# Sliding-window attention with a SwiGLU block: V loads of the opening issued behind a mask matmul, two V copies moved to VectorE

## The chip, the cores and the metric

The kernel runs on one core of a Trainium2 chip. The metric is the device time of one execution in microseconds (us). The core has TensorE (PE, matrix products), VectorE (DVE), ScalarE (ACT), GpSimd (POOL) and SyncE (SP), and 16 DMA engines that all queues share.

## The reference

```python
# q, k, v: [8, 8, 576, 64] float32 (batch, head, position, head dim)
scores = (1/8) * q @ k^T
mask   = (rel >= 0) & (rel < 64)          # rel = query position - key position
attn   = softmax(where(mask, scores, -1e9))
x      = (attn @ v) -> [4608 tokens, 512]  # tokens = batch * position, heads side by side
g      = x @ w_gate                        # [512, 1536]
out    = (g * sigmoid(g) * (x @ w_val)) @ w_out   # [1536, 512], float32
```

Each query sees its own and the 63 positions before it.

## The kernel before

The 4608 tokens are 36 chunks of 128. For each chunk n the kernel forms scores (S), takes the exponential (ACT, tile `pt`), masks, multiplies with V (AV, tile `va`), normalises (DVE, tiles `rc` and `xb`) and transposes the result into `xT` (X). Four chunks make one FFN chunk of 512 tokens: F c.f computes one 128-column group of the gate and value products with `Wg` and `Wv` (L788), tanh on ACT (`sig`, L794), and two DVE operations (`uu` L796, `hT` L798); O multiplies with `Wo` (L819).

The program is recorded as a list of operations (`_Graph.op`), each put on an engine in the order of the Python calls. `emit` then gives every engine its list and adds a semaphore wait wherever an operation reads or overwrites what another one made. So each engine runs strictly in the order of the calls. `after=` adds a wait on one more operation; `self.hold`, if set, is passed as `after` to the K, Q and V loads. Behind the opening, a written-out order (`EARLY`, `LOADS`, `SHIPS`) and a planner that picks PSUM banks take over.

All casting loads (float32 in DRAM, bf16 in SBUF) are issued from POOL: `load2` (K and Q of two chunks, L376), `load` (V, K or Q of one chunk, L367), `load_w` (two 128-column groups of a weight, L382). POOL also runs the masks' `affine_select` and some copies.

`shift(n, r, eng)` (L296 through `copy`) is the V copy of the change: the attention of chunk n needs the last 64 rows of V of the chunk before and the first 64 of its own in one tile, in the order of the scores' rows. `shift(n, r)` copies 64 rows of `va[n]` into tile `vs[n + r - 1]`: r=1 the later half for the next chunk, r=0 the first half for the chunk itself. AV of chunk 1 reads vs 0 (`shift(0,1)` and `shift(1,0)`), that of chunk 2 vs 1 (`shift(1,1)`, `shift(2,0)`), that of chunk 3 vs 2 (`shift(2,1)`, `shift(3,0)`).

`Sbias` (L449) is a pair of matmuls that puts a large negative number into the masked places of a chunk's scores, ahead of the score matmuls (`Sb`, L469 and L473). `warm` (L763) are matmuls on zeros. In the opening (`loads`, then `build` up to `self.main("F0.2-3b")`) the order is written out by hand: loads and masks, first transposes of K and Q, chunks 0 to 3 of the attention, and the first FFN groups in halves of 256 tokens.

Of the kernel before, what the change touches and what calls it, by code (L numbers as in the profile page):

```python
# [166 lines left out]
class _Kernel:  # L167
# [235 lines left out]
    def T2(self, st, x, engs):  # L403
        g = self.g
        src = (self.ks2 if x == "k" else self.qs2)[st % 2]
        dst = self.kT if x == "k" else self.qT
        z0 = (2 * st) % self.NZ
        for cc in range(2):
            bank, bk = self.bank("a")
            tb = bank[:, 0:256].bitcast(BF).rearrange("p (c j t) -> p c j t", c=2, j=2)  # L410

            def pe(e, cc=cc, tb=tb):
                for c in range(2):
                    for j in range(2):
                        for p in range(2):
                            r = e.transpose(tb[64 * p:64 * p + 64, c, j, :], src[:, 4 * cc + 2 * c + p, j, :], self.ident[:, :])  # L416
                return r

            g.op("pe", pe, reads=["ident", ("s2", x, st % 2, 0), ("s2", x, st % 2, 1)], writes=[bk])
            d = dst[:, 2 * cc:2 * cc + 2, 128 * z0:128 * z0 + 256].rearrange("p c (t j) -> p c t j", j=2)  # L420
            a = tb.rearrange("p c j t -> p c t j")
            self.copy(engs[cc], d, a, [bk], [(x + "T", z, cc) for z in (z0, z0 + 1)])
            self.drop([(bank, bk)])
# [282 lines left out]
    def X(self, n, eng="sp", kind="f", half=False):  # L706
        if n >= NCH:
            return
        g = self.g
        ix, it, u = n % 4, (n // 4) % self.NX, n % 4  # L710
        xb = self.xb[ix]
        xo = self.xT[it][:, :, 128 * u:128 * u + 128]
        xk = [("xb", ix, 0), ("xb", ix, 1)]
        if eng == "sp":
            g.op("sp", lambda e: e.dma_start_transpose(xo, xb[:, :]), reads=xk, writes=[("xT", it, u)], dma=True)
            return
        bank, bk = self.bank(kind)
        tb = bank[:, 0:256].bitcast(BF).rearrange("p (c t) -> p c t", c=4)

        def pe(e):  # L720
            for c in range(4):
                for p in range(2 if half else 1):
                    w = 64 if half else 128
                    r = e.transpose(tb[w * p:w * p + w, c, :], xb[:, 128 * c + w * p:128 * c + w * p + w], self.ident[:, :])  # L724
            return r

        g.op("pe", pe, reads=["ident"] + xk, writes=[bk])
        self.copy(eng, xo, tb, [bk], [("xT", it, u)])
        self.drop([(bank, bk)])
# [38 lines left out]
    def F(self, c, fs, lo=0, hi=512):  # L768
        g = self.g
        nf, n = len(fs), hi - lo  # L770
        w = nf * n
        xT = self.xT[c % self.NX]
        xk = [("xT", c % self.NX, u) for u in range(lo // 128, hi // 128)]
        ih = c % self.NH
        i = self.n_s % self.NS
        self.n_s += 1
        sig, uu = self.sig[i], self.uu[i]
        out = self.hT[ih][:, fs[0]:fs[0] + nf, lo:hi]
        v3 = lambda a: a[:, 0:w].rearrange("p (f t) -> p f t", f=nf)
        bs = []  # L780
        for W, wk in ((self.Wg, "Wg"), (self.Wv, "Wv")):
            bank, bk = self.bank("f")
            bs.append((bank, bk))

            def pe(e, W=W, bank=bank):
                for a, f in enumerate(fs):
                    for kk in range(NK):
                        r = e.matmul(bank[:, a * n:a * n + n], W[:, kk, f * 128:f * 128 + 128], xT[:, kk, lo:hi],  # L788
                                     start=(kk == 0), stop=(kk == NK - 1))
                return r  # L790

            g.op("pe", pe, reads=xk + [(wk, f) for f in fs], writes=[bk], cost=w * 0.0017)
            if wk == "Wg":
                g.op("act", lambda e, G=bank: e.activation(sig[:, 0:w], G[:, 0:w], ACTF.Tanh, scale=0.5), reads=[bk], writes=[("sig", i)])  # L794
        (G, gk), (V, vk) = bs
        g.op("dve", lambda e: e.scalar_tensor_tensor(uu[:, 0:w], sig[:, 0:w], 1.0, G[:, 0:w], ALU.add, ALU.mult),  # L796
             reads=[("sig", i), gk], writes=[("uu", i)])
        g.op("dve", lambda e: e.scalar_tensor_tensor(out, v3(uu), 0.5, v3(V), ALU.mult, ALU.mult),  # L798
             reads=[("uu", i), vk], writes=[("hT", ih, f) for f in fs])
        self.drop(bs)  # L800
# [61 lines left out]
    def loads(self):  # L862
        self.first_loads()
        self.load2(0, "q")
        self.load2(1, "k")
        self.load2(1, "q")
        self.init()
        self.init_ident()
        self.init_mask()
        self.init_nmask()  # L870
        for n in range(4):
            self.load(n, "v")
        self.W(0, 2)
        self.load_w("g", 2, 4)
        self.shift(0, 1, "pool")
        self.shift(1, 1, "pool")
        self.load_w("v", 2, 4)
        self.shift(2, 1, "pool")
        self.shift(3, 0, "pool")
        self.W(4, 6)  # L880
        self.W(6, 8)
# [179 lines left out]
    def build(self):  # L1061
        F, S, AV, X, T2, O = self.F, self.S, self.AV, self.X, self.T2, self.O
        self.loads()
        self.banks("a", [4, 5, 6, 7, 0, 1, 2, 3, 4, 5, 0, 1, 2, 3, 4, 5, 6, 7, 0, 1, 2, 3, 4, 5, 6, 7, 6, 7])
        self.warm(48, n=121)
        self.first_T(("dve", "act"))
        s0 = self.Sa(0)
        T2(0, "q", ("act", "dve"))
        self.Sbias(s0)
        self.warm(2)  # L1070
        self.Sb(s0)
        s1 = self.Sa(1, True)
        self.Sb(s1)
        T2(1, "k", ("dve", "act"))
        T2(1, "q", ("dve", "act"))
        self.start()
        s2, s3 = self.Sa(2), self.Sa(3)
        a0, a1, a2, a3 = self.AVa(0), self.AVa(1), self.AVa(2), self.AVa(3)
        self.AVs(a0)
        self.shift(1, 0, "dve")  # L1080
        self.AVn(a0)
        self.shift(2, 0, "dve")
        self.Sbias(s2)
        self.Sb(s2)
        self.AVs(a1)
        self.AVn(a1)
        self.Sbias(s3)
        self.Sb(s3)
        X(0, "dve", "a")
        X(1, "dve", "a")  # L1090
        self.warm(1, j=2)
        self.AVs(a2)
        self.AVn(a2)
        self.AVs(a3)
        self.AVn(a3)
        F(0, (0, 1), 0, 256)
        X(2, "act", "a")
        X(3, "act", "a")
        F(0, (2, 3), 0, 256)
        F(0, (0, 1), 256, 512)  # L1100
        for n in range(4):
            self.did |= {w % n for w in ("s%d", "a%d", "x%d", "Tk%d", "Tq%d")}
        self.main("F0.2-3b")
        self.free = set(range(8))
        self.g.now = dict.fromkeys(self.g.now, max(self.g.now.values()))
        for t in self.program():
            self.pump()
            first = len(self.g.ops)
            self.main(t)
            self.at[t] = next((o for o in self.g.ops[first:] if o.eng == "pe"), None)  # L1110
        self.pump()
        assert not any(self.queues)
        self.g.emit()
# [42 lines left out]
```

## Time and profile before

| what | value |
|---|---|
| median of three runs | 329.18 us (328.08 to 330.15) |
| the profiled execution | 327.34 us, span 325.6 us |
| PE busy | 316.7 us, 97% of the span |
| DVE, ACT, POOL busy | 62%, 42%, 33% |
| casting loads (software queue) | 18.62 MB written |
| HBM read, written | 37.75 MB, 9.44 MB |
| granted TensorE clock | 1.00 |

The span runs from the first to the last instruction of the profiled execution; the execution's time has 1.74 us around it. PE's busy share counts pipelined matmuls as busy, so 97% does not say that PE is at its peak, but that there is little time in which nothing runs on it. In the timeline a row gives start, duration, engine, line, operation, output and input; a bracket gives the idle time before it and what ended it. For a DMA issued by POOL the row is the time that POOL takes to issue it; the data land some microseconds later (the DMA view has this).

### The profile page before, as it was taken

How to read it: one execution, taken by the hardware profiler on the slowest of the kernel's cores; microseconds unless marked ns; L12 is line 12 of the kernel's file. 1: busy time of each engine (PE TensorE's matmuls, PEld its weight loads, DVE VectorE, ACT ScalarE, POOL GpSimd, SP SyncE). 2: the span in 40 equal slices, each digit the busy share in tenths (PEclk: the TensorE clock that was granted, in tenths of full speed). 3: DMA queues.
4: the chain of work that ended last, by engine and by line, in shares of the span. 5: the costliest groups of instructions: out<-in, count | busy, mean ns of one | idle time of the engine just before them, and what ended most of it. 6: DMA issues, size and time to landing. Idle time of an engine off the chain costs nothing.

```text
span 325.6 us, 8009 instructions
## 1 busy us (share of the span) xinstructions
PE 316.7 (97%) x3415; PEld 171.1 (53%) x3451; DVE 203.5 (62%) x351; ACT 135.8 (42%) x243; POOL 108.3 (33%) x138
## 2 busy tenths in 40 slices
PE   7999999999999999999999999999999999999996
PEld 7584578775455445545444454545454544444443
DVE  4777978745387819675757575666656566555520
ACT  2745864454454344342434252525252532322222
POOL 8999980007930502506060607060702000000000
PEclk9999999999999999999999999999999999999999
DMA  9999999999999993949697999999996202100012
GB/s 146 178 193 184 168 166 154 130 169 182 166 175 140 168 197 80 125 100 138 122 133 113 142 120 123 137 121 126 121 138 81 66 35 56 42 32 33 34 62 99
DMA packets 161571, 39.85 MB, mean 122 GB/s; under 512 B 148608, under 2 KB 157056, under 8 KB 161536
## 3 DMA queue, kind: packets, MB, share of 16 engines
q0 software_dynamic: 111056, 18.62, 78.6%
q1 hardware_dynamic: 45024, 11.22, 24.5%
q10 hardware_dynamic: 5456, 9.51, 8.7%
q8 instruction: 27, 0.44, 0.6%
q14 instruction: 8, 0.07, 0.1%
HBM read 37.75 MB, written 9.44 MB: 145 GB/s over the span
## 4 chain that ended last, share of the span: by engine, by line
PE 92%; ACT 3%; issue 2%; POOL 1%; DVE 1%; ACTq 0%; POOLq 0%
PE ps L788 56%; PE ps L819 28%; PE ps L642 3%; ACT pt L481 1%; PE ps L506 1%; PE ps L724 1%; PE ps L469 1%; PE ps L844 1%; PE ps L416 1%; POOL qs L376 1%; PE ps L473 1%; PE ps L593 1%; ACT kT L294 0%; ACT qT L294 0%; PE ps L510 0%
## 5 line engine op out<-in xcount | busy, mean ns | idle before, releaser
L796 DVE SCALAR_TENSOR_TENSOR uu<-sig,ps 128x512 bf16<-128x512 bf16 x108 | 73.9, 684 | 64.3 <-ACT sig L794 63.8
L788 PE MATMUL ps<-xT,Wv 128*128 128x512 bf16 (+1 forms) x486 | 110.5, 351 | 0.5
L788 PE MATMUL ps<-xT,Wg 128*128 128x512 bf16 (+1 forms) x479 | 107.8, 351 | 2.7 <-issue 1.9
L794 ACT ACTIVATE sig<-ps 128x512 bf16<-128x512 f32 x108 | 65.0, 602 | 76.2 <-PE ps L788 76.0
L819 PE MATMUL ps<-Wo,hT 128*128 128x512 bf16 x413 | 94.5, 379 | 0.5 <-issue 0.2
L798 DVE SCALAR_TENSOR_TENSOR hT<-uu,ps 128x512 bf16<-128x512 bf16 x108 | 74.2, 687 | 3.7
L788 PEld LDWEIGHTS ps<-xT,Wv 128*128 128x128 bf16 x496 | 48.5, 98 | 44.9
L367 POOL DMA_DIRECT2D kn<-in_k_dram x31 | 27.6, 894 | 127.4 <-PE ps L819 96.3
L788 PEld LDWEIGHTS ps<-xT,Wg 128*128 128x128 bf16 x496 | 46.6, 98 | 42.1 <-ACT pt L518 0.2
L819 PEld LDWEIGHTS ps<-Wo,hT 128*128 128x128 bf16 x420 | 41.0, 98 | 48.4
L826 ACT ACTIVATE ost<-ps 128x512 f32<-128x512 f32 x35 | 20.9, 597 | 88.6 <-PE ps L819 88.6
L367 POOL DMA_DIRECT2D va<-in_v_dram x40 | 35.5, 911 | 11.0 <-PE ps L819 10.9
L367 POOL DMA_DIRECT2D qn<-in_q_dram x31 | 27.9, 909 | 0.0
L669 DVE RECIPROCAL rp<-ps 128x14 f32<-128x14 f32 (+1 forms) x28 | 5.7, 203 | 31.6 <-PE ps L642 31.4
L481 ACT ACTIVATE pt<-ps 128x512 bf16<-128x512 f32 x36 | 18.9, 599 | 6.4 <-PE ps L473 6.0
L518 ACT ACTIVATE pt<-ps 128x512 bf16<-128x512 f32 x36 | 18.6, 603 | 4.3 <-PE ps L510 4.3
L671 DVE TENSOR_TENSOR xb<-ps,rp 128x896 bf16<-128x896 f32 (+1 forms) x28 | 19.4, 691 | 1.0
L642 PEld LDWEIGHTS ps<-va,pt 64*64 64x64 bf16 x888 | 10.8, 107 | 6.1 <-issue 5.5
L642 PE MATMUL ps<-va,pt 64*64 64x65 bf16 x888 | 13.4, 193 | 0.1
L527 DVE TENSOR_TENSOR pt<-pt,kmask 128x1024 bf16<-128x1024 bf16 x18 | 12.3, 684 | 0.0
L527 DVE TENSOR_TENSOR pt<-pt,mask 128x1024 bf16<-128x1024 bf16 x14 | 9.4, 686 | 0.9 <-ACT pt L481 0.9
L473 PE MATMUL ps<-qT,kT 64*64 64x64 bf16 x288 | 7.8, 195 | 0.0
(65 smaller groups left out, 139.4 us busy)
## 6 DMA issues: line engine op xcount, KB each, us to landing
out_dram<-ost ACTq DMA_DIRECT2D x35, 256.0 KB, 3.2
va<-in_v_dram POOLq DMA_DIRECT2D x32, 128.0 KB, 5.9
kn<-in_k_dram POOLq DMA_DIRECT2D x25, 128.0 KB, 5.3
qn<-in_q_dram POOLq DMA_DIRECT2D x25, 128.0 KB, 5.7
Wg<-in_moe_w_gate_dram POOLq DMA_DIRECT2D x6, 256.0 KB, 7.1
Wv<-in_moe_w_val_dram POOLq DMA_DIRECT2D x6, 256.0 KB, 7.1
Wo<-in_moe_w_out_dram POOLq DMA_DIRECT2D x2, 768.0 KB, 19.0
qs<-in_q_dram POOLq DMA_DIRECT2D x3, 256.0 KB, 6.2
```

What stands on the lines that cost most here:

```text
L367: self.g.op("pool", lambda e, d=d, a=a: e.dma_start(d, a), writes=ks, dma=True, after=self.hold)
L481: g.op("act", lambda e, po=po, p=p: e.activation(po, sv[p], ACTF.Exp, scale=SCALE), reads=[bx[p][1]], writes=[pk[p]])
L518: g.op("act", lambda e, po=po, p=p: e.activation(po, sv[p], ACTF.Exp, scale=SCALE), reads=[bx[p][1]], writes=[pk[p]])
L527: self.g.op("dve", lambda e: e.tensor_tensor(pt, pt, m, ALU.mult), reads=pk + [key], writes=pk)
L642: z = e.matmul(self.psa[64 * c:64 * c + 64, o:o + 65], pt[p][rows, h, 64 * a:64 * a + 64], va[m][rows, h, 0:65], start=first, stop=phase = ...
L671: g.op("dve", lambda e, d=d, num=num, rb=rb: e.tensor_tensor(d, num, rb, ALU.mult), reads=bk + [("rp", k)], writes=xk, cost=(1.0, 0.25)[k])
L788: r = e.matmul(bank[:, a * n:a * n + n], W[:, kk, f * 128:f * 128 + 128], xT[:, kk, lo:hi], start=(kk == 0), stop=(kk == NK - 1))
L794: g.op("act", lambda e, G=bank: e.activation(sig[:, 0:w], G[:, 0:w], ACTF.Tanh, scale=0.5), reads=[bk], writes=[("sig", i)])
L796: g.op("dve", lambda e: e.scalar_tensor_tensor(uu[:, 0:w], sig[:, 0:w], 1.0, G[:, 0:w], ALU.add, ALU.mult), reads=[("sig", i), gk], writes ...
L798: g.op("dve", lambda e: e.scalar_tensor_tensor(out, v3(uu), 0.5, v3(V), ALU.mult, ALU.mult), reads=[("uu", i), vk], writes=[("hT", ih, f) ...
L819: r = e.matmul(OB[:, :], hT[:, f, 128 * u:128 * u + 128], self.Wo[:, f, :], start=(f == 0), stop=(f == NF - 1), skip_group_check=mid is no ...
L826: g.op("act", lambda e: e.activation(ost[:, :], OB[:, :], ACTF.Copy), reads=[ok], writes=[("ost", io)])
```

## The change

V of chunks 2 and 3 and the weight loads are no longer issued with the other loads, but from a new function `next_loads`, which is called right behind `Sbias` of chunk 0. The load of V 2 gets this operation as `after`, so POOL waits there for the mask matmuls of chunk 0; what POOL issues behind it comes later in its list. `shift(0,1)` and `shift(2,1)` move from POOL to DVE, at two places in the hand-written order. The weights' order stays: columns 0-1, 2-3 and so on, gate ahead of value.

```diff
@@ loads
         self.init_nmask()
-        for n in range(4):
-            self.load(n, "v")
+        self.load(0, "v")
+        self.load(1, "v")
+
+    def next_loads(self, after):
+        self.hold = after
+        self.load(2, "v")
+        self.hold = None
+        self.load(3, "v")
         self.W(0, 2)
-        self.load_w("g", 2, 4)
-        self.shift(0, 1, "pool")
         self.shift(1, 1, "pool")
-        self.load_w("v", 2, 4)
-        self.shift(2, 1, "pool")
+        self.W(2, 4)
         self.shift(3, 0, "pool")
         self.W(4, 6)
         self.W(6, 8)
@@ build
         self.Sbias(s0)
+        self.next_loads(self.g.ops[-1])
         self.warm(2)
...
         self.AVs(a0)
+        self.shift(0, 1, "dve")
         self.shift(1, 0, "dve")
         self.AVn(a0)
...
         X(0, "dve", "a")
+        self.shift(2, 1, "dve")
         X(1, "dve", "a")
```

## The prediction

> **What bounds the kernel now.** I read the page first, then the chain of waits, then the timeline of the first 25 us, then the DMA view issue by issue.
>
> ```profile
> span 325.6 us, 8009 instructions
> ...
> PE   7999999999999999999999999999999999999996
> ...
> DMA  9999999999999993949697999999996202100012
> ...
> PE 92%; ACT 3%; issue 2%; POOL 1%; DVE 1%; ACTq 0%; POOLq 0%
> ```
>
> TensorE (PE) is on 92% of the chain that ended last, so a change counts only where PE has to start something later or may start it earlier. The DMA engines are at 9 in the first fifteen slices (about 120 us): early on there is a second queue that can become the bound. The edited code works before 25 us, so that is the stage to read. The chain there:
>
> ```profile
> 9.57 2.06 ACT pt L481 x4
> 11.64 0.49 ACT kT L294
> 12.13 0.50 ACT qT L294
> 12.67 0.22 PE ps L469
> ...
> 15.51 0.76 PE ps L593 x31
> 16.27 1.85 PE ps L788 x16
> 18.12 0.45 PE ps L724 x8
> 18.57 5.24 PE ps L788 x48
> ```
>
> ScalarE's exponentials and copies set the pace to 12.6 us; the attention of chunks 2 and 3 (L593) ends at 16.2; from there PE runs the first FFN groups (L788) without a gap. What GpSimd (POOL) does meanwhile:
>
> ```profile
> 5.38 3.79 POOL L367 DMA_DIRECT2D va<-in_v_dram  x4
> 9.14 0.78 POOL L382 DMA_DIRECT2D Wg<-in_moe_w_gate_dram  x1
> 9.88 0.78 POOL L382 DMA_DIRECT2D Wv<-in_moe_w_val_dram  x1
> 10.62 0.79 POOL L382 DMA_DIRECT2D Wg<-in_moe_w_gate_dram  x1
> 11.45 1.17 POOL L296 COPY vs<-va 64x512 bf16<-64x512 bf16 x2
> 12.55 0.74 POOL L382 DMA_DIRECT2D Wv<-in_moe_w_val_dram  x1
> 13.29 0.63 POOL L296 COPY vs<-va 64x512 bf16<-64x512 bf16 x1
> 14.13 0.61 POOL L296 COPY vs<-va 64x512 bf16<-64x512 bf16 x1 [0.21 <-DMA va<-in_v_dram]
> ```
>
> POOL issues, copies, and waits once, 0.21 us, for V of chunk 3. The DMA view, asked for the issue at 12.55 alone, gives the tightest transfer:
>
> ```profile
> Wv<-in_moe_w_val_dram POOLq DMA_DIRECT2D x1, 256.0 KB, 6.6
> ```
>
> 12.55 + 6.55 (unrounded) = 19.11 us, and PE's matmuls on these weights (Wv of columns 2 to 3) start at 19.28: 0.17 us of slack. In the same way Wg 0-1 lands at 15.07 (used at 16.20), Wv 0-1 at 16.42 (17.09) and Wg 2-3 at 17.81 (18.41). The next ones, Wg 4-5 and Wv 4-5, land 2.8 us or more ahead.
>
> **The change, part by part.**
>
> (a) V of chunk 2 waits for the mask bias of chunk 0 (L449). That pair of matmuls starts at 8.12 and ends at 8.72 in the timeline; with 0.13 us for the semaphore, POOL goes on at about 8.85. V 0 and V 1 still go out at 5.38 and 6.28. V 2 was issued at 7.41, so it moves by 1.44 us. Behind the waiting instruction stand, in POOL's order, V 3, Wg and Wv 0-1, the copy for chunk 1, Wg and Wv 2-3, the copy for chunk 3, and every later load; with the same issue times as before (0.87 per V, 0.74 per weight pair) V 3 goes at 9.72, Wg 0-1 at 10.58, Wv 0-1 at 11.32, Wg 2-3 at 12.7 (it now has one copy, 0.61, ahead of it), Wv 2-3 at 13.45 (two copies stood ahead of it, now one). The order of all DMAs is unchanged; SP's, ScalarE's and TensorE's lists are the same in both builds.
>
> What decides is not the issue but whether the DMA queue runs dry. In the packet records the first V load's packets run from 8.58, the second's to 10.57, and the third's begin at 10.54: back to back, saturated from 4.5 us to 44. After the change the third starts at 8.85 plus the time from issue to first packet. This is not shown for an issue to an emptied queue in mid-kernel, so it is bounded. Nearest row: the first load of the same queue, issued at 1.32 into an empty queue, has its first packet at 3.96:
>
> ```profile
> q1 hardware_dynamic: 174, 0.18, 58.7%
> q10 hardware_dynamic: 162, 0.15, 46.6%
> q0 software_dynamic: 2, 0.00, 0.5%
> ```
>
> (the DMA view for 3 to 4 us: the software queue has two packets by 4.0.) That is 2.64 us. Above: V 0, 5.38 to 8.58, 3.20 us, which holds queueing too. Below: the hardware queue's first load, 0.82 to about 2.4, 1.6 us. At 2.64 packets begin at 11.5, so the queue stands idle for 0.95 us; at 3.20, 1.5; at 1.6, 0. I take 2.64, the same queue and the same kind of transfer. Behind the gap the queue is again back to back (V 3's packets could start at 12.36, V 2's end at about 12.37), so every landing shifts by 0.95, Wv 2-3 to 20.06. With the semaphore PE starts on it at 20.12 instead of 19.28: +0.84 us. Part of it shows earlier, on Wv 0-1 (17.37 against 17.09).
>
> A page states a shorter time: the Trainium skill, "DMA: Bandwidth & Descriptors", section Specifications, puts the first byte of a DMA issued by GpSimd at about 1 us. By it the queue would not run dry and the weights would cost nothing; the trace's 2.64 us disagrees, and the sum goes by the trace.
>
> (b) Two copies move from POOL to VectorE (DVE): 2 x 0.61 off POOL, two more of the 64x512 form on DVE, one ahead of the normalisation of chunk 0 (12.04), one between the two xT copies (15.0). DVE is nearly without a gap there:
>
> ```profile
> 12.04 0.72 DVE L296 COPY vs<-va 64x512 bf16<-64x512 bf16 x1
> 12.68 0.19 DVE L609 RECIPROCAL rc<-ps 128x8 f32<-128x8 f32 x1
> 12.90 0.69 DVE L612 TENSOR_TENSOR xb<-ps,rc 128x512 bf16<-128x512 f32 x1
> 13.51 0.56 DVE L296 COPY vs<-va 64x512 bf16<-64x512 bf16 x1
> ...
> 15.02 0.81 DVE L296 COPY xT<-ps 128x512 bf16<-128x512 bf16 x2
> ```
>
> Dear end: each costs its start-to-start time, 0.48 to 0.64, together 1.1 us, less the 0.3 between the last xT copy (15.83) and its use (16.20) and 0.1 of idle before 15.02: FFN starts 0.7 late. Cheap end: both DVE copies of before end 0.14 and 0.15 us after a POOL copy ends (12.62 to 12.76, 13.92 to 14.07), so most of their time may be waiting, and a copy by itself may cost 0.15. Then the first lot ends no later than now (POOL has one copy there instead of two), the second, at 15.2, can be held by POOL's copy for chunk 3, and FFN starts about 0.1 late. The floor under the start does not move: chunk 3's attention needs the exponentials that end at 15.78.
>
> The Trainium skill, "SBUF — State Buffer", section Who interferes with whom, speaks for the cheap end: a VectorE copy in a two-port mode and a GpSimd instruction lock a shared port pair, and the later one blocks wholly. The two 0.15 us remainders agree with that. By it this term is 0.1, by the durations 0.7.
>
> I take 0.1 to 0.7 without choosing: both lie under the 0.84 of (a). The terms are not added, since a late FFN start makes the weights' wait shorter.
>
> (c) POOL's copy for chunk 3 waits for V 3: landing 14.08 + 0.95 = 15.03, copy to 15.65, still ahead of 15.78. Behind it Wg 4-5 goes at about 15.65 (14.69 before), first packet 18.3, while the queue is fed until 17.69 + 0.95 = 18.64: no second gap, by 0.3 us. From there loads are 0.95 later and PE 0.84: the tightest of them, K of the chunk pair 6-7, lands at 35.90 with 0.95 in hand, of which 0.11 goes.
>
> **Sum.** 0 (DVE, covered) + 0.84 (Wv 2-3), never regained, since PE is the chain from there: span 326.4. The profiled run's own time is 327.34, 1.74 around the span, so 328.2. The median shown is 329.18, 1.84 above the profiled run; on its scale 330.0.
>
> **Rivals.**
> 1. The queue does not run dry (1.6 us or less to the first packet) and the copies are cheap: one mechanism, the cover by transfers already queued. It decides where V 2's packets appear before 10.6. Price 0 to 0.1: 329.2, not slower. For it: three loads are queued at 8.85. Against: 2.64 on this very queue. Nothing that it frees is waited for by PE, so a real gain is not in the trace.
> 2. The DVE copies are dear and the gap is small: FFN starts 0.7 late, weights never late: 329.9, told from mine by the place of the idle time (before 16.9, not at 17 to 20).
> 3. A second gap: V 3 lands later still (3.2 us to the first packet gives 1.5 of shift), POOL stands before its copy until 15.6, and Wg 4-5 starts a dry queue again. Price 1.35 at Wv 2-3, up to 0.6 more where the slack of the K pair is used up: 330.5 to 331.1.
> 4. PE's clock falls back during the stalls. The 48 warm-up matmuls of 121 columns took 4.81 us, 0.100 each, 1.2 columns per ns; FFN runs 512 in 0.217, 2.4 per ns. Another 5 us at half rate costs 2.5: 332.5, over 1% slower. It decides if PE's pauses are long; they are some 0.3 and 0.5 us, and pauses of 0.4 to 0.6 us between 6 and 16 us led to none.
>
> **How the numbers follow.** Forecast 0.55 (330.0), rival 1 0.2, rival 2 0.1, rival 3 0.1, rival 4 0.03, else 0.02. The causes span 329.2 to 331.1; three runs of one kernel differ by 2 us (328.08 to 330.15), so I add 0.9 below and 0.3 above: 328.3 to 331.4. A measurement of this kernel tells about 1% (3.3 us) from no change; only rival 4 and unforeseen things reach that: slower 0.05, faster 0.03, within 0.92.
>
> **What would show it.** Right: V 2's issue at 8.8 to 8.9; POOL idle 1.4 us before it; a hole of 0.7 to 1.1 us in the DMA row between 10.5 and 11.6; PE idle ahead of L788 between 17 and 20.2, together with the later start 0.8 us; Wg 4-5 used 0.8 late, with no idle ahead of it; the rest parallel. Wrong: no hole (rival 1), PE idle before 16.9 only (rival 2), matmuls of 256 columns at 0.22 instead of 0.11 us apart (rival 4), or a PE idle behind 25 us that before does not have.

## The result, and the profile after

| | median (all runs) | profiled execution | span |
|---|---|---|---|
| before | 328.35 us (327.21 to 332.19, 14 runs) | 327.34 us | 325.6 us |
| after | 330.03 us (328.58 to 334.95, 14 runs) | 329.81 us | 328.1 us |

The ratio is 1.0053, with a 95% interval of 1.0028 to 1.0078: slower by 1.74 us (0.9 to 2.6). It leaves out one much slower execution of each kernel (332.19 and 334.95), so that it stands for medians of 328.08 and 329.82. That is inside 1%, but it is a loss that the measurement tells from none. A second measurement of the same kernel (e11, below) gave 1.0048 (1.0027 to 1.0070). The two profiled executions are 2.5 us apart, more than the ratio says.

The page after, in the same rows as before (span, busy tenths, the chain that ended last by engine):

```profile
span 328.1 us, 8042 instructions
...
DMA  9999999999999994979999999999997111100012
...
PE 90%; DMA 4%; POOL 2%; DVE 1%; ACT 1%; issue 1%; POOLq 0%
```

PE had 92% of the chain before and no DMA was named in it; now DMA has 4% of it. The DMA row alone shows no hole. The chain from 5 us on (start, duration, what; cut where it says "...") says which transfers these are:

```profile
6.28 6.10 DMA va<-in_v_dram
...
12.43 0.61 POOL vs L296
13.04 0.67 POOL Wg L382
13.72 7.17 DMA Wv<-in_moe_w_val_dram
...
20.93 9.72 PE ps L788 x64
```

The last part is the one that counts: Wv 2-3, issued at 13.72, lands at 20.88 (19.11 before), and PE takes it at 20.93. POOL's timeline (start, duration, engine, line, operation; the bracket is the idle time ahead and what ended it):

```profile
9.02 1.75 POOL L367 DMA_DIRECT2D va<-in_v_dram  x2 [1.60 <-PE ps L449]
10.75 0.77 POOL L382 DMA_DIRECT2D Wg<-in_moe_w_gate_dram  x1
```

The wait on L449 is there, 1.60 us long. It ends 0.30 us after the mask matmuls (8.72). PE's timeline at the first FFN groups:

```profile
16.46 1.05 PE L788 MATMUL ps<-xT,Wg 128*128 128x256 bf16 x8
17.42 1.05 PE L788 MATMUL ps<-xT,Wv 128*128 128x256 bf16 x8
...
19.59 1.05 PE L788 MATMUL ps<-xT,Wg 128*128 128x256 bf16 x8 [0.68 <-DMA Wg<-in_moe_w_gate_dram]
20.93 1.05 PE L788 MATMUL ps<-xT,Wv 128*128 128x256 bf16 x8 [0.29 <-DMA Wv<-in_moe_w_val_dram]
```

Against before these four start 0.26, 0.33, 1.18 and 1.65 us later. From there to 90 us PE runs 1.65 us behind, without another wait. Then comes one that nobody had on the list:

```profile
96.79 0.24 PE L469 MATMUL ps<-qT,kT 64*64 64x128 bf16 x2 [0.98 <-DVE hT L798]
```

The score matmuls of a later pair wait about 1 us. The releaser named, `hT`, had long been done; what landed just then (96.70) is the transpose of Q that SP issues. Before, it landed at 93.36 and was used 0.6 us later. With this PE runs 2.5 us behind, to the end.

The copies on DVE:

```profile
12.15 1.04 DVE L296 COPY vs<-va 64x512 bf16<-64x512 bf16 x2
13.95 0.27 DVE L296 COPY vs<-va 64x512 bf16<-64x512 bf16 x1
15.41 0.55 DVE L296 COPY vs<-va 64x512 bf16<-64x512 bf16 x1
```

The first row is two copies, one of 0.29 and one of 0.73; the second runs beside POOL's copy of V 1 (12.43 to 13.04). The copy at 13.95 takes 0.27. The one at 15.41 takes 0.55 with no POOL copy beside it; POOL is issuing a load then.

### The profile page after: what moved, and what is told of

Read it like the earlier page. It is cut to its first block, busy times and chain, and to the rows that moved or that the text cites. A ratio compares the mean times of both kernels' runs of the same rounds, so it can differ in the third digit from the quotient of the medians.

```text
span 328.1 us, 8042 instructions
## 1 busy us (share of the span) xinstructions
PE 320.1 (98%) x3451; PEld 170.2 (52%) x3451; DVE 203.9 (62%) x353; ACT 136.0 (41%) x243; POOL 107.2 (33%) x136
## 4 chain that ended last, share of the span: by engine, by line
PE 90%; DMA 4%; POOL 2%; DVE 1%; ACT 1%; issue 1%; POOLq 0%
PE ps L788 56%; PE ps L819 28%; PE ps L642 3%; DMA Wv<-in_moe_w_val_dram 2%; DMA va<-in_v_dram 2%; PE ps L506 1%; PE ps L844 1%; PE ps L469 1%; POOL qs L376 1%; PE ps L724 1%; DVE uu L796 0%; DVE hT L798 0%; PE ps L416 0%; PE ps L473 0%; ACT sig L794 0%
## 5 line engine op out<-in xcount | busy, mean ns | idle before, releaser
L788 PE MATMUL ps<-xT,Wg 128*128 128x512 bf16 (+1 forms) x496 | 111.3, 352 | 0.8 <-DMA Wg<-in_moe_w_gate_dram 0.7
L819 PE MATMUL ps<-Wo,hT 128*128 128x512 bf16 x420 | 95.4, 379 | 0.0
L819 PEld LDWEIGHTS ps<-Wo,hT 128*128 128x128 bf16 x420 | 41.0, 98 | 48.5
L826 ACT ACTIVATE ost<-ps 128x512 f32<-128x512 f32 x35 | 20.9, 597 | 88.6 <-PE ps L819 88.6
L671 DVE TENSOR_TENSOR xb<-ps,rp 128x896 bf16<-128x896 f32 (+1 forms) x28 | 19.4, 692 | 1.0
L469 PE MATMUL ps<-qT,kT 64*64 64x128 bf16 x144 | 7.1, 219 | 1.0 <-DVE hT L798 1.0
## 6 DMA issues: line engine op xcount, KB each, us to landing
Wo<-in_moe_w_out_dram POOLq DMA_DIRECT2D x2, 768.0 KB, 20.9
```

Source lines behind the costliest of these rows:

```text
L671: g.op("dve", lambda e, d=d, num=num, rb=rb: e.tensor_tensor(d, num, rb, ALU.mult), reads=bk + [("rp", k)], writes=xk, cost=(1.0, 0.25)[k])
L819: r = e.matmul(OB[:, :], hT[:, f, 128 * u:128 * u + 128], self.Wo[:, f, :], start=(f == 0), stop=(f == NF - 1), skip_group_check=mid is no ...
L826: g.op("act", lambda e: e.activation(ost[:, :], OB[:, :], ACTF.Copy), reads=[ok], writes=[("ost", io)])
```

## The experiments

Two theories at first. Q: the wait on L449 makes the software DMA queue late, and the weights of columns 2 to 3 come late. V: the copies on DVE hold up the first attention chunks. "Lag" below is how much later than in before the same tanh on ACT (`sig`) runs, by the traces; every kernel has one trace. The control of each comparison is the kernel before, run on the same chip. Ratios have their 95% interval. A load's semaphore is raised 16 times, once by each DMA engine: the "first report" of a load is the first of these, and it has landed with the last.

**e1: without the wait, copies on DVE as changed.**

```diff
-        self.hold = after
         self.load(2, "v")
-        self.hold = None
```

> V of chunk 2 is issued without the wait for the mask matmuls; the two copies stay on VectorE, the order of all issues is that of the changed kernel. Theory Q (the wait lets the DMA queue run thin, so Wg and Wv 2-3 land late): V 2 is issued at 7.4 us again, Wg 2-3 lands before 18.0 and Wv 2-3 before 19.4, no idle time of TensorE at L788 before 25 us, and the time is that of before within 0.2% (ratio 0.998 to 1.002). Theory V (the two copies on VectorE cost the time): FFN starts at about 16.5 instead of 16.2 as in the changed kernel and the ratio stays at 1.003 or above. Theory C (the late landings of the changed profile are chance of one slow DMA engine, not of the wait): ratio like the changed kernel's own only by chance, landings late here too.

Ratio 1.0010 (0.9988 to 1.0032). V 2 goes out at 7.41 again. Wv 2-3 has its first report at 17.65 (17.67 in before) but lands at 19.62, later than the 19.4 expected: the last engine reports 0.5 us further behind the first than in before, though there is no wait on L449. PE waits for no weights. FFN starts 0.68 us late all the same, but the chain to it does not go through the copies: PE stood still in the scores of chunk 3 on "issue", that is, on nothing that the profile shows:

```profile
14.86 0.22 PE L473 MATMUL ps<-qT,kT 64*64 64x64 bf16 x2 [0.66 <-issue]
```

The lag stays 0.67, to the end. The two copies therefore do not explain the loss (e12, below, has them too and no lag).

**e2: the wait alone, copies on POOL as before.**

```diff
-        for n in range(4):
-            self.load(n, "v")
+        self.load(0, "v")
+        self.load(1, "v")
+
+    def next_loads(self, after):
+        self.hold = after
+        self.load(2, "v")
+        self.hold = None
+        self.load(3, "v")
...
         self.Sbias(s0)
+        self.next_loads(self.g.ops[-1])
```

> The wait and the later issue alone; all six copies of the opening as before (four on GpSimd). Theory Q: the wait alone gives the whole loss, ratio 1.004 to 1.009, TensorE idle at L788 for Wg or Wv 2-3. It may be a little more than the changed kernel, since the copy for chunk 1 on GpSimd now stands behind the later issues (first copy about 13.0 instead of 11.45), so that FFN starts at 16.9 or later. Theory V: without the two copies on VectorE the ratio is 1.002 or less.

Ratio 1.0036 (1.0016 to 1.0055), a little under the 1.004 to 1.009 expected. The chain:

```profile
9.03 1.75 POOL va L367 x2
...
12.23 8.16 DMA Wg<-in_moe_w_gate_dram
...
20.43 1.59 PE ps L788 x13
```

Here Wg 2-3 is the late one (20.39), with 1.31 us of idle on PE; the lag is 2.04 by 21 us. Its first report is 0.94 late, the rest is the last engine, 3.11 us behind the first (1.47 in before). The wait alone brings the loss: theory V falls as its cause, Q stands.

**e3: cover for the wait.** The weights 0-1 are issued ahead of the waiting V 2, so that 2.7 us of transfers lie in the queue.

```diff
         self.load(1, "v")
+        self.W(0, 2)
...
         self.load(3, "v")
-        self.W(0, 2)
```

> The changed kernel with Wg and Wv 0-1 issued ahead of the wait, so that two transfers of 1.34 us each are queued while GpSimd waits; V 2 and V 3 then land about 2.7 us later. Theory Q: the queue stays full, Wg 2-3 and Wv 2-3 land as before the change (17.8 and 19.1, give or take a slow engine's 1.4), no idle time of TensorE for them; what may remain is chunk 2's and 3's attention waiting for V: V 3 lands at about 15 to 16.5, GpSimd's copy ends 0.65 later, FFN starts at 16.3 to 17.6; ratio 1.000 to 1.004. Theory V: as the changed kernel, 1.003 to 1.008.

A miss: 1.0099 (1.0064 to 1.0134). The weights were on time (Wv 2-3 at 19.03, no idle ahead of it), but now V 2 and V 3 stand behind them, and land at 15.53 and 16.37. DVE, in its timeline, waits for V 2:

```profile
15.56 0.28 DVE L296 COPY vs<-va 64x512 bf16<-64x512 bf16 x1 [1.74 <-DMA va<-in_v_dram]
```

POOL waits 2.77 us for V 3, FFN starts 1.71 late, and PE again has an "issue" stall, 1.07 us. The cover did not remove the lateness, it gave it to the transfers that stand behind it.

**e4: a longer wait** (on the score matmuls of chunk 1, so V 2 goes out at 10.75), and **e7: the same with eight `warm` matmuls** in PE's pauses.

```diff
-        self.next_loads(self.g.ops[-1])
...
         s1 = self.Sa(1, True)
         self.Sb(s1)
+        self.next_loads([o for o in self.g.ops if o.eng == "pe"][-1])
```

e7 has besides:

```diff
         self.shift(2, 1, "dve")
+        self.warm(4, j=2)
         X(1, "dve", "a")
...
         self.AVn(a3)
+        self.warm(4, j=6)
         F(0, (0, 1), 0, 256)
```

> The wait is put on the score matmuls of chunk 1 (end at about 10.5 us) instead of the mask matmuls of chunk 0 (8.7), so V 2 and all behind it are issued 1.7 us later still. Theory Q: the hole in the DMA queue grows by 1.7 us, every landing shifts by as much, FFN groups 2-3 start 1.7 us later than in the changed kernel: ratio 1.009 to 1.013 to before. Theory V or C: no more than 0.5 us beyond the changed kernel, ratio 1.007 at most.

> The kernel with the wait on the score matmuls of chunk 1, and eight more matmuls on zeros put into TensorE's two pauses before FFN (four ahead of the transpose of chunk 1, four ahead of the first FFN group). Theory K (in that kernel FFN groups 0-1 ran at half rate, 0.21 us for 256 columns, because the pauses let the clock fall back, and this cost 1.7 of its 3.7 us): with the pauses filled the groups run at 0.11 us, FFN 2-3 then waits for its weights (landing about 22.2) instead: 0.5 to 1.2 us better than without, ratio 1.006 to 1.008. If the clock does not depend on the pauses: half rate again and 1.010.

e4: 1.0099 (1.0073 to 1.0125). By another way than a late Wv 2-3: FFN starts at 18.33 instead of 16.20, and its first 16 matmuls then run at half rate, 1.86 us for 8 instead of 1.05. PE's timeline, and then a row of the table by stretch (window, its length, busy time of PE, PEld, DVE, ACT, POOL with counts, granted clock, DMA share, GB/s):

```profile
18.33 1.86 PE L788 MATMUL ps<-xT,Wg 128*128 128x256 bf16 x8 [1.01 <-DMA Wg<-in_moe_w_gate_dram]
19.99 1.87 PE L788 MATMUL ps<-xT,Wv 128*128 128x256 bf16 x8
```

```profile
18.33:22.00 3.67, 3.67 (x22) 2.61 (x23) 0.88 (x3) 0.60 (x1) 3.67 (x6) 0.54 1.40 186
```

The granted clock is 0.54 in that stretch (0.5 from 18.28 to 21.69, 1.0 on either side). Ahead of it, from 14.70 to 18.33, PE was busy for 1.47 of 3.63 us, in three pauses of 0.95, 0.21 and 1.01 us and smaller ones. In e7, busy for 3.30 of 4.40 us there, the clock stays at 1.00 and 8 matmuls take 1.03 to 1.05. The ratio, 1.0069 (1.0037 to 1.0101), is the one expected, but its interval overlaps that of e4, and the trace shows no gain: the lag is 3.80 (3.74 in e4), with 0.42, 0.21 and 0.29 us of waits for Wg 0-1, Wv 0-1 and Wv 2-3 (landing at 23.03). In this trace PE at full rate merely reaches the late weights sooner. The Trainium skill, "TensorE: Matmul & The Clock Gate", Part 1, gives about 3.4 us of idle as what takes PE back to half rate; in e4 pauses of about 1 us, with light work between them, were enough.

**e6: a shorter wait** (on the transposes of Q, which end at 8.19; V 2 goes out at 8.49).

```diff
-        self.next_loads(self.g.ops[-1])
+        self.next_loads([o for o in self.g.ops if o.eng == "pe"][-2])
```

> The wait is put one TensorE operation earlier, on the transposes of Q of chunks 0 and 1 (end 8.19 us) instead of the mask matmuls (8.72). V 2 is then issued at about 8.45 and its first packet, 1.4 to 2.1 us later as in the traces with the wait, comes at 9.9 to 10.6, when V 1 is just done (10.6 to 11.1). Theory Q with a threshold: the queue hardly runs dry, so nearly no loss: ratio 1.000 to 1.003. If the loss goes with the lateness of the issue alone, without a threshold, it is two thirds of the changed kernel's: 1.003 to 1.004.

Ratio 1.0005 (0.9966 to 1.0044): too wide to say much. By the trace Wv 2-3 lands at 20.00, PE waits 0.22 us for Wv 0-1 and 0.32 for Wv 2-3, and the lag is 0.78, then 1.17 by 38 us, where the K load comes 0.20 late. The first report of Wv 2-3 is 0.56 late where it is 1.08 late in after. The profiled execution (332.4 us) also has "issue" stalls of 0.65 us at 71.27 and 3.04 us at 89.85, which the other traces do not have and whose cause stays open.

**e5: the late weights not needed at once.** The first 256 tokens of groups 2 to 3 are multiplied with columns 0 to 1; all loads stay.

```diff
-        bs = []
+        bs, ws = [], (0, 1) if (c, fs, lo) == (0, (2, 3), 0) else fs
...
-                for a, f in enumerate(fs):
+                for a, f in enumerate(ws):
...
-            g.op("pe", pe, reads=xk + [(wk, f) for f in fs], writes=[bk], cost=w * 0.0017)
+            g.op("pe", pe, reads=xk + [(wk, f) for f in ws], writes=[bk], cost=w * 0.0017)
```

> The changed kernel, but the first 256 tokens of FFN groups 2-3 are computed with the weight columns 0-1, which have landed, so TensorE does not wait for Wg and Wv 2-3 there (the loads themselves stay, and the second half of the tokens uses the right columns). Theory Q (the loss is the wait for those late weights): the idle time ahead of L788 at 19 to 21 us is gone, what is left is the FFN start of the changed kernel (16.5 to 16.9, 0.3 to 0.7 late): ratio 0.999 to 1.003. Theory L (a good part of the loss arises later, between 90 and 110 us, where scores wait for K and Q transposed by DMA): ratio 1.003 to 1.005 in spite of it.

Ratio 1.0030 (0.9994 to 1.0066), between no loss and all of it. In the trace the wait at 19.6 to 20.9 is gone and the lag is only 0.37 behind the first groups. It then grows to 0.84 at 37.66, where the transposes of K (L416) wait 0.28 us for their load, and to 2.7 behind waits at L469 of 0.98 and 0.70 us at 96 and 106. So a consumer that is moved away saves its own wait, but the stream of loads is still late and meets the next tight one, here the K load of the opening. The waits at 96 and 106 are not shown to come from that stream: the loads that these scores need go out behind a pause of POOL of 27 to 30 us, which a PE operation (L819) ends at 75 to 79 us in every trace, so they are issued as late as PE is.

**e8: no wait, all six copies on DVE.**

```diff
-        self.hold = after
         self.load(2, "v")
-        self.hold = None
...
-        self.shift(1, 1, "pool")
...
-        self.shift(3, 0, "pool")
...
+        self.shift(1, 1, "dve")
...
+        self.shift(3, 0, "dve")
```

> No wait, and all six V copies of the opening on VectorE, so that GpSimd only issues. A VectorE copy by itself took 0.28 to 0.29 us from start to end in the traces where GpSimd stood still. Expected: five copies of about 0.3 us or less on VectorE, Wg 2-3 and later weights issued 1 to 3 us earlier than without the wait, no copy blocked by GpSimd. If VectorE's list sets the FFN start, it is 0.3 to 0.6 late: ratio 1.001 to 1.002; if GpSimd's copies had been holding up VectorE, 0.998 to 1.000.

Ratio 1.0026 (0.9995 to 1.0056). The weights are early (Wv 2-3 at 18.93), but FFN starts 1.55 late, not 0.3 to 0.6: PE waits 0.71 us for `xb` and 0.71 for the copy for chunk 3. Three of the six copies take 0.28 to 0.29, the others 0.54 to 0.62, though POOL makes no copy at all. DVE has room for two more copies (e12, below), not for four. This trace also has a late wait, 1.12 us at 106.53, where the Q transpose is named, and no wait on L449: the late wait can come without the change.

**e9 and e10: fewer loads.** Wg and Wv 2-3 are not loaded, groups 2 and 3 are computed with columns 0 to 1; e9 in the changed kernel, e10 in the kernel before.

```diff
-        bs = []
+        bs, ws = [], [f - 2 if f in (2, 3) else f for f in fs]
...
-                for a, f in enumerate(fs):
+                for a, f in enumerate(ws):
...
-            g.op("pe", pe, reads=xk + [(wk, f) for f in fs], writes=[bk], cost=w * 0.0017)
+            g.op("pe", pe, reads=xk + [(wk, f) for f in ws], writes=[bk], cost=w * 0.0017)
...
-        self.W(2, 4)
```

(e9; in e10 the last line is the two `load_w` of columns 2 to 4.)

> The changed kernel without the loads of the weight columns 2 to 3 (Wg and Wv, two transfers of 256 KB); groups 2 and 3 of the FFN are computed with the columns 0 to 1 instead, so this part of the output is left out. Theory S (the change costs what it costs because the whole stream of loads is 1.2 to 1.4 us late, and each tight transfer behind it passes that on to PE): with 2.7 us of transfers taken out of the stream, every load behind them has more slack than the wait takes, so the wait costs nothing here; PE starts the FFN 0 to 0.3 us later than in the control and stays that much behind; ratio 0.998 to 1.001, and within 0.001 of the control. Rival T (the wait costs PE something that is not the stream: code, clock, order): ratio 0.004 to 0.005 above the control, as between the two kernels of the case.

> The control: the kernel before with the same two loads left out, groups 2 and 3 computed with the columns 0 to 1. Both theories: no transfer is late before either, so 0.998 to 1.001.

e9 1.0037 (1.0007 to 1.0066), above what theory S allows, e10 1.0016 (0.9989 to 1.0044): 0.002 apart with intervals that overlap, so the times do not decide between S and T. The traces speak for S: the spans are 325.7 and 325.3, and the lag is +0.31 and -0.21 at 43 us, +0.09 and -0.33 at the end. Half of the 0.5 is a Wv 0-1 that lands at 17.34 in e9 and holds PE up, the other half an earlier FFN start in e10. With 2.7 us of transfers taken out, the wait costs 0.5 us at 43 us in place of 1.65, and neither trace has a wait at L469.

**e11: the changed kernel once more.**

> The changed kernel once more, for its ratio beside the two others and for a second trace: 1.003 to 1.008. If the wait for transposed K or Q at 94 to 107 us belongs to the change, it is in this trace too, some 0.7 to 1 us; if it comes and goes, the lag of PE stays at 1.6 to 1.7 us from 20 us to the end.

Ratio 1.0048 (1.0027 to 1.0070). PE's timeline has one wait in place of two, to nearly the same lag (1.80):

```profile
21.07 1.05 PE L788 MATMUL ps<-xT,Wv 128*128 128x256 bf16 x8 [1.13 <-DMA Wv<-in_moe_w_val_dram]
```

The late wait at L469 is there too (1.40 us at 97.41), and takes the lag to 3.15.

**e12: V 2 ahead of the wait, V 3 behind it.**

```diff
         self.load(1, "v")
+        self.load(2, "v")

     def next_loads(self, after):
         self.hold = after
-        self.load(2, "v")
+        self.load(3, "v")
         self.hold = None
-        self.load(3, "v")
```

> The changed kernel with V 2 issued ahead of the wait; V 3 is now the load that waits for the mask matmuls. Theory S: one more load of 256 KB lies in the queue over the wait. V 3 goes out at about 9.0 and has its first packet at about 11.1 (2.06 us on), while V 2's packets last to about 11.4 as before, so no hole; Wv 2-3 is issued at about 13.0, and lands at 19.1 to 19.7; PE waits at most 0.3 us for it, and the lag is 0.3 to 0.7 us: ratio 1.000 to 1.0025. Rival T: the wait is there as before, so 1.004 to 1.006.

Ratio 1.0009 (0.9990 to 1.0028). (A V load writes 128 KB, by the DMA view; 256 KB is what it reads.) The wait is still there (V 3 goes out at 9.02, the weights 0-1 at 9.89 and 10.63), but V 2 is in the queue ahead of it, and the queue's rate falls from 155 only to 141 GB/s, for 1 us. Wv 2-3 lands at 19.11, exactly as before. The chain:

```profile
16.07 1.86 PE ps L788 x16
...
18.37 5.33 PE ps L788 x48
```

FFN starts a little earlier than before (the first `sig` by 0.20 us), with both copies on DVE. The loss is gone although wait and copies stay: what costs is that the queue had too little in it when the wait began. The loads behind V 2 also go out 0.6 to 0.9 us earlier than in after, which e12 does not tell apart from the fuller queue; but e1, which issues the weights 0-1 another 0.75 us earlier, gains only 0.22 us at the first report of Wv 2-3. The lag is -0.29 at 86 us and +0.45 behind 0.47 us of idle at L469, put to "issue".

The kernels that differ in when V 2 goes out, in one table (us; first reports and landings from the traces' semaphore records):

| kernel | V 2 issued | Wv 2-3, first report | Wv 2-3 lands | lag at 25 us |
|---|---|---|---|---|
| before | 7.41 | 17.67 | 19.11 | 0 |
| e12 (V 3 waits) | 7.41 | 17.87 | 19.11 | -0.1 |
| e1 (no wait) | 7.41 | 17.65 | 19.62 | 0.7 |
| e6 | 8.49 | 18.23 | 20.00 | 0.8 |
| after, e11, e2 | 9.02, 9.03, 9.03 | 18.75, 19.17, 18.84 | 20.88, 21.02, 21.12 | 1.65, 1.80, 2.0 |
| e4, e7 | 10.75 | 20.99, 20.95 | 22.17, 23.03 | 3.7, 3.8 |

No version beats the kernel before; e12, e1 and e6 are not told from it.

## Why the prediction was right or wrong

**The class and the number.** Within 1% was right, and that 330.0 meets 330.03 is luck. The effect forecast was +0.84 us; measured is +1.74 (0.9 to 2.6). The base of three runs, 329.18, came out at 328.35 in 14 runs: the base was 0.83 too high and the effect about as much too low.

**(a), the place: right.** V 2 waits, V 3 and all weights go late, and PE waits for columns 2 to 3 between 17 and 21 us. e1 against e2 shows the wait as the cause, e12 that it acts through the queue.

**(a), the first step that failed: "What decides is not the issue but whether the DMA queue runs dry", and with it "the queue stands idle for 0.95 us".** The issue came at 9.02, not 8.85: 0.30 us behind the mask matmuls where I took 0.13. (The trace of before had the row: POOL's load at 75.49 starts 0.31 us behind the end, at 75.18, of the PE operation that it waits for.) The time to the first packet was not 2.64 either. e4 and e7 show it for what the prediction could not find, an issue to an emptied queue in mid-kernel. In the DMA view of e4 for 10.5 to 13.5 us, in 40 slices of 0.075 us:

```profile
DMA  9997542333100000000000002595999999999999
GB/s 318 73 60 49 33 27 17 20 20 20 9 0 0 0 0 0 0 0 0 0 0 0 0 0 14 38 60 34 72 97 133 137 133 154 145 152 159 137 142 101
```

By the packet records the software queue has no packet from 11.32 to 12.33, and V 2, issued at 10.75, begins there: 1.58 us (1.59 in e7; the 318 holds an instruction fetch). By that time V 2 of after, issued at 9.02, would begin at 10.60, while the packets ahead of it last to 10.5 in before and to 11.1 in after. So the queue does not run dry, and by the prediction's own rule the weights would have cost next to nothing. The DMA view of after for 8.9 to 15 us has the rate in 40 slices of 0.15 us:

```profile
GB/s 162 167 166 165 155 157 152 160 158 154 144 229 87 118 129 132 133 147 121 117 124 101 108 149 128 76 72 95 116 137 153 170 191 174 171 175 185 181 188 191
```

No slice is at zero; from 10.7 us on the rate is about 120 for nearly 3 us (the 229 holds an instruction fetch). Worked out from the packet records, the software queue alone in GB/s, by half microseconds:

| from (us) | 10.0 | 10.5 | 11.0 | 11.5 | 12.0 | 12.5 | 13.0 | 13.5 |
|---|---|---|---|---|---|---|---|---|
| before | 156 | 155 | 156 | 155 | 166 | 190 | 193 | 194 |
| after | 154 | 114 | 131 | 128 | 116 | 101 | 114 | 174 |
| e2 | 142 | 80 | 110 | 106 | 107 | 117 | 121 | 159 |
| e12 | 155 | 156 | 154 | 148 | 141 | 157 | 182 | 195 |

In place of a short hole there is a long shallow one, which the sum has no term for. From 10.5 to 13.5 us after moves 156 KB less than before (0.5 us times the sum of the differences, 311), 0.8 us at the later 190 GB/s, and 0.1 us more by 15.5. The first reports agree: those of Wg 0-1, Wv 0-1, Wg 2-3 and Wv 2-3 come 0.99, 1.01, 1.05 and 1.08 us later than before. That the shift of 0.95 was near this is luck, since the hole that it was worked out from was not there. A reason why it stays shallow for so long can be read in POOL's row: V 2, V 3 and Wg 0-1 go out 0.86 and 0.87 us apart, and in before a V load drains in 0.85. A queue that is fed no faster than it drains does not fill up again; only the weights, 256 KB in 0.74 us of issue, build up stock. That the rate in the trough is lower still than one V load (128 KB) in 0.87 us, which would be 150 GB/s, is not explained by this, and stays open.

**(a), the second step that failed: "so every landing shifts by 0.95".** It held for the weights 0-1, which landed 0.96 and 0.95 later. Those of columns 2-3 landed 1.74 and 1.77 later, and PE was 1.65 behind in place of 0.84. The difference is the last of the 16 engines, a term that the prediction put at nothing. In after it reports 1.37 us behind the first for Wv 0-1 (1.43 in before), but 2.17 for Wg 2-3 (1.47) and 2.13 for Wv 2-3 (1.44): 0.7 us. That this part belongs to the change is not shown. For Wv 2-3 the last engine is 1.85 behind in e11 and 2.28 in e2, but only 1.18 in e4; without the wait it is 1.97 in e1 and 1.28 in e8.

**The page weighed against the trace.** The Trainium skill, "DMA: Bandwidth & Descriptors", Specifications, has about 1 us to the first byte; by it the weights would have cost nothing. Measured from the start of the issue, the first packet comes after 1.58 and 1.59 us on the emptied queue (e4, e7), and for Wg 0-1, the one transfer of after, e11 and e2 whose first packet its size tells from those ahead, after 2.20, 2.16 and 1.88 in a thin queue. So the time lies between the page's and my 2.64, but what cost something was the trough, which neither figure gives.

**(b), the copies: right, at the cheap end.** FFN started 0.26 late with 0.1 to 0.7 forecast, 0.2 early in e12. What I read as 0.15 us for a copy alone is 0.27 to 0.29. Which half of the range held could be read from the two DVE copies that ended just behind POOL's. The Trainium skill's port lock ("SBUF — State Buffer", Who interferes with whom) agrees with the copy of after that starts 0.02 us behind a POOL copy: it takes 0.73 and ends 0.15 behind that copy. POOL's copies are not the whole of it. In after and e8 four DVE copies of 0.54 to 0.62 us have no POOL copy beside them; each ends about 0.1 us behind the end of a load's issue by POOL (15.95 behind 15.86; 13.00, 14.48 and 16.59 behind 12.89, 14.37 and 16.47). A copy that lies inside an issue (13.95 to 14.22 in after, the issue 13.72 to 14.52) takes 0.27. So moving copies off POOL does not free them of POOL; the reason is argued from these ends alone.

**(c), no second gap: right.** Wg 4-5's packets follow those of Wv 2-3, and its users do not wait. "From there loads are 0.95 later and PE 0.84: the tightest of them ..." held in kind to 44 us (K of the chunk pair 6-7 lands 1.78 later, PE is 1.65 behind and does not wait) and not beyond: the transposes at 96 us, 0.6 us of slack, were not looked at. "A PE idle behind 25 us that before does not have" was on the list of what would make the prediction wrong, and it came. It accounts for 0.8 us of the 2.5 between the profiled executions, and for 1.35 in e11.

**The rivals.** 1: its condition came true, the queue never runs dry, and by e4 the time to the first packet is its 1.6; its price, nothing, was wrong, since PE waits. 2 fell (the idle time is at 19 to 21 us). 3 did not happen, though its price came close to what was seen: the lateness grew without a second gap. 4 did not happen in this change; e4 shows it with pauses of 0.95, 0.21 and 1.01 us.

**What stays open.** Why the late transposes are missed at 94 to 107 us. A wait at L469 shows there in the traces of after, e2, e3, e5, e7, e11 and e12 (0.4 to 1.4 us at a time, some of them put to "issue"), but also in e8 with no wait on L449, and e4, among the latest of all, has none. And how often an execution has it: the ratios (about 1.7 us) lie nearer to the lag at 25 us than to the profiled executions' 2.5 and 3.2, so perhaps not always; this was not shown.

## What to carry to other kernels

Price a later issue by what lies in the queue when it happens, not by the gap alone: a queue that never runs dry can still lose a microsecond, where the issuing engine feeds it no faster than it drains. One more transfer ahead of the wait can cover it (e12), if the order stays as the consumers need it: e3 put the weights ahead and lost more at V. Give the last engine of a transfer a term of its own: here it was 1.2 to 2.3 us behind the first for the same load, from trace to trace. And when a stream of loads is late, follow it past the first consumer that waits: taking that one away (e5) left the K load at 37 us to wait for.

## What the runs showed of the hardware that was not expected

- A queue that runs thin need not stop: in after it runs at 100 to 130 GB/s instead of 155 to 190 for 3 us, and the busy share of the DMA engines stays at 9 tenths all the while. So the hole in the DMA row that the prediction named as its sign did not appear there; the row in GB/s has the trough. In e4, with V 2 issued 1.7 us later still, the queue does empty, and both rows show it.
- Issue to first packet on the software queue in mid-kernel: 1.58 and 1.59 us on an emptied queue (e4, e7), 1.88 to 2.20 in a thin one (e2, e11, after); 2.64 for the first load of the program.
- Half the granted clock for 3.4 us after pauses of 0.95, 0.21 and 1.01 us within 3.6 us (e4); matmuls on zeros in these pauses kept it at 1.00 (e7).
- PE stood still on "issue" for 0.66 us in e1 and 1.07 us in e3 at about 14 us, at a place where before has 0.15. The first 16 KB instruction fetch behind the start lies at 12.50 in e1 and 12.90 in e3. It lies at 11.64 to 11.98 in e12, e10, e8 and before, and at 10.56 to 11.23 in e4, after, e2 and e11, none of which has such a stall: a thinner queue of loads goes with an earlier fetch. That the fetch waits behind the loads, and PE for the fetch, is argued from these starts, not shown.
- The second fetch begins at 16.66 us in after, in the midst of Wg 2-3's packets (16.19 to 17.66), where the last engine falls from 1.37 to 2.17 us behind the first. In before the same happens at V 3, from 0.45 to 1.76, whose packets the first fetch (11.98) falls among. These two fetches take 1.05 and 0.96 us. They may be what holds up the last engine; the packet records do not name the engine, so this stays open.
